# Attention and a gated layer on one core: weight conversion and gram matrices rearranged, order of work searched anew

## The chip, the cores and the metric

One core of a Trainium2 chip runs the whole program. The metric is device time in microseconds of one execution. Engines: PE (matrix multiplication, with its weight loads PEld), DVE (vector), ACT (scalar), POOL (GpSimd), SP (issues the DMAs).

## The reference

Causal attention for 4 batches of 12 heads, 448 positions and head width 64, then a gated two-layer network over the 1792 tokens:

```python
scores = scale * np.matmul(q, k.transpose(0, 1, 3, 2))      # scale = 1/sqrt(64)
scores = np.where(mask, -1000000000.0, scores)              # causal
attn = np.exp(scores - np.max(scores, axis=-1, keepdims=True))
attn = attn / (np.sum(attn, axis=-1, keepdims=True) + 1e-09)
attn_out = np.matmul(attn, v)
x = attn_out.transpose(0, 2, 1, 3).reshape(1792, 768)
h = x @ w_in                                                # w_in 768 x 2048
g = h * (1.0 / (1.0 + np.exp(-1.702 * h)))
return g @ w_out                                            # w_out 2048 x 768
```

w_in and w_out arrive as 64-bit floating-point words, q, k and v as 32-bit ones.

## The kernel before

**Tiling.** Each batch is cut into two blocks of rows (256 and 192 positions), eight blocks in all. Heads are worked in pairs ("units", six a block). For the first batch attention is computed in float32: k and q are turned on PE (`turn`, line 893), scores go to PSUM (line 412), the softmax runs strip by strip of 64 rows (`chunk`, lines 1112 and 1126), the probabilities are turned on PE (line 883) and multiplied with v (line 1268). Later batches use pairs of float16 values, high part and remainder, that DMA transposes turn. A block's result is `xT` (high part and remainder, line 477). The gated layer takes a block at a time: `h_slice` multiplies eight slices of w_in (256 columns each) with `xT`, three products each (line 412, tile `ps_h`), ACT takes the tanh (line 1362), DVE forms the gate (line 1367) and splits it into `gT`; `out_tile` multiplies `gT` with w_out (line 1405, tile `ps_o`).

**Weights.** Before a slice of w_in or a pair of row groups of w_out can be used, its 64-bit words are loaded and turned into float32 by four passes (`to_f32`): a scaling of the upper words (line 472 on ACT), the low 13 shifted bits (line 574 on DVE or 566 on ACT), the sign bit (line 588, DVE only), and their union with the shifted upper word (line 599, DVE). A gram matrix on PE gives squares whose largest value, found by `tensor_reduce` on DVE (line 628), yields a power of two as scale; the same instruction takes the maximum over all partitions once `all_max` has spread the column on PE. Then ACT or DVE writes the high part in float16 (lines 472 and 474) and DVE the remainder (line 477): eight pairs `wib`, sixteen pairs `wob`. Slices 0 to 2 of w_in are converted in two halves of 768 columns, slices 3 to 7 in one piece of 1536. Gram matrices of v of the first batch, of w_in and of w_out are built of blocks of 128 columns: two matmuls, each with 64 stationary and 128 moving columns.

**What sets the order.** The code records operations with costs by engine, buffers read and written (`Ops.add`). `Ops.order` plans a forward pass over the five engines with these costs, takes the finishing times, plans backward with noise added to them, and repeats this 600 times; `scored` rates a plan, and the best one becomes the order on every engine. Where an operation lists two engines the plan also chooses the engine. Tile's own scheduling is off (`manual_schedule`), so a changed cost or a changed search moves instructions on all engines.

Of the kernel before, what the change touches and what calls it, by code (L numbers as in the profile page):

```python
# [48 lines left out]
    va=2,  # L49
    ub=(0.0, 60.0, 122.92, 9.75),  # L50
    wi2=2.63,
    early=3,
)

SEED = 2
# [2 lines left out]
class Ops:  # L58
# [8 lines left out]
    ENGINES = ("SP", "PE", "ACT", "DVE", "POOL")  # L67
    HOP = 0.14
    SECOND = 1e5
    LOAD = 0.68  # L70
    DMA_START, DMA_END, DMA_DEPTH = 1.23, 1.6, 8
    ROWS = 0.195

# [24 lines left out]
        deps.discard(me)  # L98
        self.ops.append((costs, fn, sorted(deps), prio, dma))

    ROUNDS, STEPS, SPREAD = 600, 6, (0.0, 0.5, 1.0, 2.0)

    def order(self):
        rnd = Random(SEED)
        best = now = self.scored([o[3] for o in self.ops])
        bad = 0
        for _ in range(self.ROUNDS):
            spread = rnd.choice(self.SPREAD)
            now = self.scored(self.backward(now, spread, rnd))
            if now[0] < best[0]:  # L110
                best, bad = now, 0
            else:
                bad += 1
                if bad % self.STEPS == 0:
                    now = best
        Ops.last = best[0]
        return best[1]
# [24 lines left out]
            free[e] = end[i]  # L142
        return max(free.values())

    def backward(self, found, spread, rnd):
        _, result, fin = found
        n = len(self.ops)
        on = dict(result)
        key = [-fin[i] - (rnd.gauss(0.0, spread) if spread else 0.0) for i in range(n)]
        wait, left = [0] * n, [0.0] * n  # L150
        for o in self.ops:
            for d in o[2]:
                wait[d] += 1
        ready = {e: [] for e in self.ENGINES}
        free = dict.fromkeys(self.ENGINES, 0.0)
        coming = [(0.0, i) for i in range(n) if not wait[i]]
        heapify(coming)
        at, now, done = [0.0] * n, 0.0, 0
        while done < n:
            while coming and coming[0][0] <= now + 1e-9:  # L160
                _, i = heappop(coming)
                heappush(ready[on[i]], (key[i], i))
            moved = False
            for e in self.ENGINES:
                if free[e] > now + 1e-9 or not ready[e]:
# [20 lines left out]
        return [end - x for x in left]  # L186
# [110 lines left out]
def dve(n, ap=0, rate=1.042):  # L297
    return {"DVE": (rate * n + 68 + 61 * ap) / 1e3}
# [14 lines left out]
def kernel(  # L313
# [13 lines left out]
    P = 128  # L327
# [44 lines left out]
    cols = cp.tile([P, 176], F32, name="cols")  # L372
    waste = cp.tile([P, 512], BF16, name="waste")
    one16 = cp.tile([P, P], BF16, name="one16")
    ps_s, ps_s_r = bufs(2, [P, 512], F32, "ps_s", pp)
    ps_v = pp.tile([P, 2, 256], F32, name="ps_v")
    ps_h, ps_h_r = bufs(3, [P, 512], F32, "ps_h", pp)
# [12 lines left out]
    def col(tag, n=2, w=1):  # L390
        if tag not in col_at:
            col_at[tag] = (col_used[0], Ring(n))
            col_used[0] += n * w
            assert col_used[0] <= 175
        o, ring = col_at[tag]
        i = ring.next()
        return cols[:, o + i * w : o + (i + 1) * w], ("col", tag, i)
# [11 lines left out]
    def halves(out, lhsT, rhs, start, stop):  # L409

        for o in range(0, P, 64):
            nc.tensor.matmul(out[o : o + 64], lhsT[:, o : o + 64], rhs, start=start, stop=stop)  # L412

    def all_max(src, src_key, tag, turn, prio):

        if turn == "S":
            sb = ps_s_r.next()
            row, row_keys = ps_s[sb][:, :P], [("S", sb, x) for x in range(2)]  # L420
        else:
            row, row_keys = ps_o[1][:, :P], [("O", 1)]
        top = src.bitcast(BF16)[:, 1:2].to_broadcast([P, P])
        add(
            {"PE": 0.056},
            lambda e: halves(row, top, one16, True, True),
            [src_key, "one16"], row_keys, prio,
        )
        dst, key = col(tag + "_all", 2)
        gram_max(row, row_keys[0], dst, key, prio)  # L430
        return dst, key

    def norm_scale(tag, sq, sq_key, s, s_key, inv, inv_key, prio, near=False):
# [71 lines left out]


    def consts(e):
        nc.gpsimd.memset(one16, 1.0)
        nc.gpsimd.affine_select(
            out=one16, in_=one16, pattern=[[-1, P]], compare_op=ALU.is_equal, fill=0.0, base=0, channel_multiplier=1  # L510
# [40 lines left out]
    def to_f32(k, f, raw, raw_keys, dst, dst_keys, prio):  # L551
# [11 lines left out]
        def low(e):  # L563
# [9 lines left out]
            else:  # L573
# [12 lines left out]
        add(
            dve(n, rate=0.521),
            lambda e: nc.vector.tensor_scalar(
                out=words(dst, U16, 2)[..., 1],
                in0=words(raw, U16, 4)[..., 3],  # L590
                scalar1=0x8000,
                scalar2=None,
                op0=ALU.bitwise_and,
            ),
            raw_keys, dst_keys, prio,
        )
        add(
# [11 lines left out]
    def gram(x, keys, ps, ps_key, first, last, prio):  # L609


        t = x.bitcast(BF16).rearrange("p k (m n t) -> p k m n t", n=P, t=2)[..., 1]
        blocks = [(k, m) for k in range(t.shape[1]) for m in range(t.shape[2])]

        def mm(e):
            for k, m in blocks:
                halves(
                    ps[:, :P], t[:, k, m], t[:, k, m],
                    first and (k, m) == blocks[0],
                    last and (k, m) == blocks[-1],  # L620
                )

        add({"PE": len(blocks) * 0.0585}, mm, keys, [ps_key], prio)

    def gram_max(ps, ps_key, sq, sq_key, prio):
        add(
            dve(P),
            lambda e: nc.vector.tensor_reduce(out=sq, in_=ps[:, :P], axis=AX.X, op=ALU.max),
            [ps_key], [sq_key], prio,
        )  # L630

# [253 lines left out]
    def turn(src, r, keys, prio):  # L885
# [8 lines left out]
                        ps_t[64 * j : 64 * j + 64, o : o + r], src[:r, j, t], ident[:r, :r], start=True, stop=True  # L894
                    )

        add({"PE": 2 * (4 * r / 2.4 + 5) / 1e3}, mm, keys + ident_keys, [("T", h)], prio)
        return ps_t[:, 256 * h : 256 * h + 2 * r].rearrange("p (t x) -> p x t", t=2), ("T", h)

    def k_unit32(u, c0, c1, prio):  # L900
# [170 lines left out]
    def scores_of(n, u, run, qt, qt_key, prio):  # L1071
# [23 lines left out]
                        )  # L1095

        if f32(b, u):
            add({"PE": (4 * o / 2.4 + 6 * len(run)) / 1e3}, scores32, [qt_key] + kt_keys, bank(sb), prio)
        else:
            add(  # L1100
                {"PE": 2 * (o / 2.4 + 3 * len(run)) / 1e3}, scores, [qt_key] + kt_keys, bank(sb), prio
            )
# [52 lines left out]
    def p_turned(n, run, pi, pp_i, where, rs, r_key, prio):  # L1155
# [11 lines left out]
        for tiles in groups:  # L1167
# [6 lines left out]
            def mm(e, tiles=tiles, ps=ps, p0=p0):  # L1174
# [1 line left out]
                    flip_over(ps[:, (at - p0) * P : (at - p0 + 1) * P], z_of(i)[:, J])  # L1176

            add(
                {"PE": (nt * 60 + 2 * 93) / 1e3},
                mm,  # L1180
                ident_keys + [k for i in {t[3] for t in tiles} for k in z_keys(i)], [("H", hb)], prio,
            )
# [351 lines left out]
```

## Time and profile before

| | |
|---|---|
| runs shown | 603.24, 604.72, 606.03 us (median 604.72) |
| profiled execution | 605.29 us, span 603.5 us |
| PE, DVE, ACT, POOL busy | 575.1, 416.6, 351.6, 59.2 us |
| granted clock of TensorE, mean | 0.994 |

The span runs from the first to the last instruction of the profiled execution; its own time is 1.8 us longer. Matmuls are pipelined and their ends are modelled, so that PE's busy time counts overlapping matmuls once and says little about the rate; starts of consecutive groups do. DVE and ACT durations also overlap at their ends: the rows' durations add up to more than the busy time.

### The profile page before, as it was taken

Reading aid. Unit: us, or ns where it says so; the run is one execution under the profiler, and the core shown is the slowest. Engines: PE = TensorE matmul, PEld = TensorE weight load, DVE = VectorE, ACT = ScalarE, POOL = GpSimd, SP = SyncE. Lnnn points to the kernel's source line nnn. Section 1 sums busy time; section 2 is a strip of 40 time slices with the busy share of each in tenths; the row PEclk is TensorE's granted clock in tenths of the full one; section 3 lists DMA queues with packets and bytes.
Section 4 is the critical chain, followed back from the end, with each engine's and each line's share of the span. In section 5 each row is a group of like instructions: output and inputs, shape, how many; then the busy total and the mean of one; then the engine's idle time right before and its main releaser. Section 6 shows DMA issues by size and latency. Waiting matters only on the chain.

```text
span 603.5 us, 22259 instructions
## 1 busy us (share of the span) xinstructions
PE 575.1 (95%) x9526; PEld 501.7 (83%) x9526; DVE 416.6 (69%) x1164; ACT 351.6 (58%) x835; POOL 59.2 (10%) x162
## 2 busy tenths in 40 slices
PE   3876999999999999999999999999999999999997
PEld 2555867886699799977888899998999999889986
DVE  2999999999996889977489887978777122203100
ACT  4888899887866767754676465666355122203110
POOL 3000000012120121212111210211100000000000
PEclk9989899999999999999999999999999999999999
DMA  8998478554498987899997899575835400000000
GB/s 270 277 288 281 128 251 302 173 127 110 86 177 156 142 163 112 167 176 153 156 158 115 155 161 174 105 128 120 130 59 68 94 2 15 1 28 3 28 28 27
DMA packets 201604, 79.90 MB, mean 132 GB/s; under 512 B 182304, under 2 KB 191264, under 8 KB 201504
## 3 DMA queue, kind: packets, MB, share of 16 engines
q1 hardware_dynamic: 201504, 78.47, 61.5%
q8 instruction: 74, 1.21, 0.9%
q14 instruction: 26, 0.21, 0.1%
HBM read 41.68 MB, written 5.51 MB: 78 GB/s over the span
## 4 chain that ended last, share of the span: by engine, by line
PE 68%; DVE 4%; ACT 2%; DMA 1%; issue 1%; SPq 0%; DVEq 0%; ACTq 0%
PE ps_o L1405 33%; PE ps_h L412 26%; PE ps_s L1089 4%; PE ps_v L1268 4%; DVE z L1112 1%; DMA vraw<-in_v_dram 1%; ACT p L472 1%; PE ps_s L412 1%; DVE p L477 1%; PE ps_h L883 1%; DVE ps_h L1367 0%; ACT waste L462 0%; DMA kf<-in_k_dram 0%; DVE q L477 0%; DVE gT L477 0%
## 5 line engine op out<-in xcount | busy, mean ns | idle before, releaser
L412 PE MATMUL ps_h<-xT,wib 128*64 128x256 f16 (+1 forms) x4608 | 244.4, 260 | 0.1
L1405 PE MATMUL ps_o<-wob,gT 128*64 128x384 f16 x2688 | 239.8, 326 | 0.8 <-DVE wob L477 0.6
L412 PEld LDWEIGHTS <-wib 128*64 128x64 f16 x4608 | 226.3, 110 | 7.9 <-issue 2.1
L1405 PEld LDWEIGHTS <-gT 128*64 128x64 f16 x2688 | 171.8, 110 | 38.3 <-issue 3.2
L1126 ACT ACTIVATE z<-z,cols 128x320 f32<-128x320 f32 (+6 forms) x168 | 84.1, 501 | 51.6 <-DVE cols L1112 49.1
L1367 DVE SCALAR_TENSOR_TENSOR ps_h<-t,ps_h 128x512 f32<-128x512 f32 (+1 forms) x64 | 40.1, 626 | 82.4 <-ACT t L1362 82.0
L1362 ACT ACTIVATE t<-ps_h,cols 128x512 f32<-128x512 f32 (+1 forms) x64 | 40.3, 629 | 72.1 <-PE ps_h L412 68.0
L1112 DVE CUSTOM_DVE_ANT_0 z<-ps_s,mask,cols 128x128 f32<-128x128 f32 (+6 forms) x126 | 57.2, 479 | 18.0 <-PE ps_s L1089 17.4
L477 DVE SCALAR_TENSOR_TENSOR p<-z,cols,p 128x128 f16<-128x128 f32 (+3 forms) x126 | 63.2, 528 | 1.5 <-ACT p L472 0.8
L477 DVE SCALAR_TENSOR_TENSOR gT<-ps_h,gT 128x512 f16<-128x512 f32 (+1 forms) x64 | 39.7, 620 | 13.5 <-ACT gT L472 13.1
L1268 PE MATMUL ps_v<-PT,v 128*64 128x192 f16 (+7 forms) x792 | 44.7, 257 | 0.5 <-DVE cols L453 0.4
L1089 PE MATMUL ps_s<-kT,qT 128*64 128x64 f16 (+4 forms) x504 | 41.5, 273 | 1.2 <-DVE cols L1112 0.9
L472 ACT ACTIVATE p<-z,cols 128x384 f16<-128x384 f32 (+3 forms) x66 | 34.0, 533 | 13.3 <-DVE cols L1235 9.7
L472 ACT ACTIVATE gT<-ps_h 128x512 f16<-128x512 f32 (+1 forms) x53 | 28.9, 545 | 20.4 <-DVE ps_h L1367 20.3
L472 ACT ACTIVATE ob<-ps_o,cols 128x384 f32<-128x384 f32 x24 | 13.8, 577 | 45.0 <-PE ps_o L1405 44.6
L1126 ACT ACTIVATION_READ_ACCUMULATOR z<-z,cols 128x1 f32 x168 | 31.6, 188 | 0.0
L412 PE MATMUL ps_s<-kT,qT 128*64 128x320 f32 (+6 forms) x168 | 25.0, 409 | 5.6 <-DVE cols L1112 5.6
L1268 PEld LDWEIGHTS <-v 128*64 128x64 f16 x648 | 29.2, 110 | 1.0
L1089 PEld LDWEIGHTS <-qT 128*64 128x64 f16 x504 | 24.7, 110 | 4.3 <-issue 1.3
L1047 POOL TENSOR_SCALAR q<-q 128x512 f16<-128x512 f16 (+1 forms) x32 | 21.9, 686 | 50.8 <-ACT q L472 26.6
L474 DVE TENSOR_SCALAR p<-z,cols 128x256 f16<-128x256 f32 (+3 forms) x60 | 24.6, 422 | 1.3
L472 ACT ACTIVATE wob<-wob 128x768 f32<-128x768 f32 (+1 forms) x20 | 21.8, 1091 | 5.5 <-DMA wob<-in_moe_w_in_dram 5.0
(98 smaller groups left out, 564.9 us busy)
## 6 DMA issues: line engine op xcount, KB each, us to landing
wob<-in_moe_w_in_dram SPq DMA_DIRECT2D x16, 768.0 KB, 6.5
wob<-in_moe_w_out_dram SPq DMA_DIRECT2D x9, 768.0 KB, 6.2
vraw<-in_moe_w_out_dram SPq DMA_DIRECT2D x7, 768.0 KB, 6.7
out_dram<-ob SPq DMA_DIRECT2D x28, 192.0 KB, 2.2
kf<-in_k_dram SPq DMA_DIRECT2D x36, 112.0 KB, 3.3
vraw<-in_v_dram SPq DMA_DIRECT2D x9, 384.0 KB, 5.0
qf<-in_q_dram SPq DMA_DIRECT2D x48, 64.0 KB, 3.1
qf<-in_q_dram SPq DMA_DIRECT2D x48, 48.0 KB, 3.2
```

The costliest lines, as they stand in the source:

```text
L412: nc.tensor.matmul(out[o : o + 64], lhsT[:, o : o + 64], rhs, start=start, stop=stop)
L472: nc.scalar.activation(out=dst, in_=src, func=AF.Copy, scale=sc)
L474: nc.vector.tensor_scalar(out=dst, in0=src, scalar1=sc, scalar2=None, op0=ALU.mult)
L477: nc.vector.scalar_tensor_tensor(out=dst, in0=src, scalar=sc, in1=hi, op0=ALU.mult, op1=ALU.subtract)
L1047: nc.gpsimd.tensor_scalar(out=dst, in0=src, scalar1=1.0, scalar2=1.0, op0=ALU.mult, op1=ALU.mult)
L1089: nc.tensor.matmul(ps[64 * j : 64 * j + 64], qt[:, g, i - c0, 64 * j : 64 * j + 64], kt[:, : i + 1, 64 * j : 64 * j + 64], start=(g == 0), ...
L1112: lambda e: nc.vector.tensor_tensor_reduce(out=z[:, :w], in0=ps, in1=mask[:, S - w :], scale=c, scalar=3.0e38, op0=ALU.add, op1=ALU.min, a ...
L1126: lambda e: nc.scalar.activation(out=z[:, :w], in_=z[:, :w], func=AF.Exp, bias=m, scale=-1.0, accum_out=l),
L1268: nc.tensor.matmul(ps[64 * j : 64 * j + 64, 64 * (first - c0) : w], vt[:, J, j] if f32(b, u) else vt[:, gv, J, j, :], (p_f32(pi)[:, at] if ...
L1362: lambda e: nc.scalar.activation(out=th, in_=ph, func=AF.Tanh, scale=ts[:, sl : sl + 1]),
L1367: lambda e: nc.vector.scalar_tensor_tensor(out=ph, in0=th, scalar=1.0, in1=ph, op0=ALU.add, op1=ALU.mult),
L1405: nc.tensor.matmul(po[64 * j : 64 * j + 64, :OH], gT[:, f, gg, 64 * r : 64 * r + 64], wo_pair(f, gw, nh), start=(f == 0 and gg + gw == 0), ...
```

## The change

The sign pass of `to_f32` can be planned on ACT too (a copy of the scaled upper words to float16 in place of the masked bit). Gram matrices are built of blocks of 64 columns, and their maxima are taken over 64 columns. For k of the later batches and for w_out the maximum over partitions is replaced by a sum: PE multiplies a matrix of ones with the column, and the scale's first step reads the sum in PSUM. All slices of w_in are converted in two halves. The search has 800 rounds and puts noise on the finishing times of one stretch of the plan at a time; the costs of an issue on SP (0.68 to 0.5), of turns and of float32 scores on PE differ.

```diff
-    early=3,
+    early=8,
...
-    LOAD = 0.68
+    LOAD = 0.5
...
-    ROUNDS, STEPS, SPREAD = 600, 6, (0.0, 0.5, 1.0, 2.0)
+    ROUNDS, STEPS = 800, 3
+    WHOLE, STRETCH, SPREAD, EARLY = 30, (3.0, 6.0, 12.0, 25.0), (1.0, 2.0, 4.0, 8.0), 160.0
...
-        for _ in range(self.ROUNDS):
-            spread = rnd.choice(self.SPREAD)
-            now = self.scored(self.backward(now, spread, rnd))
+        for x in range(self.ROUNDS):
+            fin = now[2]
+            if x % 4 != 3:
+                if x < self.WHOLE:
+                    lo, hi, spread = 0.0, 1e9, rnd.choice((0.0, 0.5, 1.0, 2.0))
+                else:
+                    lo = rnd.uniform(-10.0, self.EARLY)
+                    hi, spread = lo + rnd.choice(self.STRETCH), rnd.choice(self.SPREAD)
+                fin = [f + rnd.gauss(0.0, spread) if lo < f < hi else f for f in fin]
+            now = self.scored(self.backward(now[1], fin))
...
+    def total(out, src):
+        for o in range(0, P, 64):
+            nc.tensor.matmul(out[o : o + 64], ones16, src, start=True, stop=True)
...
+        if tag in ("k", "wo"):
+            half = src.bitcast(BF16)[:, 1:2]
+            add(
+                {"PE": 0.03},
+                lambda e: total(row[:, :1], half),
+                [src_key, "one16"], row_keys, prio,
+            )
+            return row[:, :1], row_keys[0]
...
+        def sign(e):
+            if e == "ACT":
+
+                nc.scalar.activation(
+                    out=words(dst, F16, 2)[..., 1], in_=words(raw, F32, 2)[..., 1], func=AF.Copy
+                )
+            else:
...
         add(
-            dve(n, rate=0.521),
...
+            {**dve(n, rate=0.521), **act(n, rate=1.0)},
+            sign,
...
-                halves(
-                    ps[:, :P], t[:, k, m], t[:, k, m],
...
+                for o in range(0, P, 64):
+                    x = t[:, k, m, o : o + 64]
+                    nc.tensor.matmul(
+                        ps[o : o + 64, :64], x, x,
...
-    def gram_max(ps, ps_key, sq, sq_key, prio):
+    def gram_max(ps, ps_key, sq, sq_key, prio, n=64):
...
-        add({"PE": 2 * (4 * r / 2.4 + 5) / 1e3}, mm, keys + ident_keys, [("T", h)], prio)
+        add({"PE": (2 * (4 * r / 2.4 + 5) + 50) / 1e3}, mm, keys + ident_keys, [("T", h)], prio)
...
-                {"PE": (nt * 60 + 2 * 93) / 1e3},
+                {"PE": (nt * 109 + 150) / 1e3},
```

Line numbers of the changed kernel are higher: 412 became 420, the gram matmuls stand at 649, 472, 474 and 477 became 492, 494 and 497, 574 and 566 became 595 and 587, 588 became 614 (DVE) and 610 (ACT), 599 became 629, 628 became 659.

The first place is PE at the end of the first gram matrix of w_in. Before:

```order
L412 LDWEIGHTS wob
L412 MATMUL ps_o_98<-wob 64x128
L412 LDWEIGHTS cols
L412 MATMUL ps_o_98<-one_90,cols 64x128
L412 LDWEIGHTS cols
L412 MATMUL ps_o_98<-one_90,cols 64x128
L893 MATMUL ps_o_97<-ident,qf 64x128 x4
```

And now:

```order
L649 LDWEIGHTS wob
L649 MATMUL ps_o_98<-wob 64x64
L420 MATMUL ps_s_91<-kT_67,qT_77 64x64 x2
L420 MATMUL ps_s_91<-kT_67,qT_77 64x128 x2
L420 MATMUL ps_s_92<-kT_67,qT_77 64x192 x2
L420 MATMUL ps_s_92<-kT_67,qT_77 64x256 x2
```

The gram matmuls write 64 columns, and the first scores now stand between the gram matrix and the pair that spreads its maximum.

The second place is DVE around the third remainder of `xT` (block 0, the last that the first matmuls of h need). Before, from row 161 of DVE on:

```order
L439 TENSOR_SCALAR cols<-cols 128x1 x2
L477 SCALAR_TENSOR_TENSOR wib<-wob,cols,wib 128x6x256
L628 TENSOR_REDUCE cols<-ps_o_98 128x1
L446 TENSOR_SCALAR cols<-cols 128x1
L453 TENSOR_SCALAR cols<-cols 128x1 x2
L477 SCALAR_TENSOR_TENSOR xT_65<-ps_v,cols,xT_65 128x512
L628 TENSOR_REDUCE cols<-ps_o_98 128x1
```

Now, from row 149 on:

```order
L614 TENSOR_SCALAR wob<-wob 128x768
L659 TENSOR_REDUCE cols<-ps_o_98 128x1
L629 SCALAR_TENSOR_TENSOR wob<-wob 128x768 x2
L659 TENSOR_REDUCE cols<-ps_o_98 128x1
L473 TENSOR_SCALAR cols<-cols 128x1
L466 TENSOR_SCALAR cols<-cols 128x1
L459 TENSOR_SCALAR cols<-cols 128x1
L497 SCALAR_TENSOR_TENSOR xT_65<-ps_v,cols,xT_65 128x512
```

The remainder of `xT` moved from row 166 to row 156; the remainder of w_in's fourth slice (`wib`), which stood ahead of it, follows it now, and both conversions of a slice in halves lie before it.

The third place is ACT at the start of the program, where the first slices of w_in are converted. Before:

```order
L472 ACTIVATE wob<-wob 128x768
L566 ACTIVATE wob<-wob 128x768
L472 ACTIVATE qT_77<-ps_o_97 64x4x64
L472 ACTIVATE wob<-wob 128x768
L566 ACTIVATE wob<-wob 128x768
L472 ACTIVATE kT_67<-ps_o_97 128x256 x2
```

And now:

```order
L492 ACTIVATE wob<-wob 128x768
L587 ACTIVATE wob<-wob 128x768
L610 ACTIVATE wob<-wob 128x768
L492 ACTIVATE wob<-wob 128x768
L492 ACTIVATE qT_78<-ps_o_97 64x4x64 x2
L492 ACTIVATE wob<-wob 128x768
L587 ACTIVATE wob<-wob 128x768
L610 ACTIVATE wob<-wob 128x768
```

Seven of the 32 halves have their sign words on ACT (L610), six of them before the first tanh.

## Rows read from the trace of the kernel before

**Rows 1.** Stretch, length; busy us of PE, PEld, DVE, ACT, POOL; clock, DMA, GB/s.
```profile
0.00:20.00 20.00, 9.85 (x98) 7.49 (x98) 8.63 (x27) 10.99 (x23) 4.54 (x22) 1.00 0.92 279
20.00:70.00 50.00, 39.04 (x552) 28.51 (x552) 48.05 (x150) 41.76 (x99) 0.00 (x0) 0.93 0.90 264
70.00:130.00 60.00, 58.05 (x946) 48.63 (x942) 59.15 (x128) 56.89 (x102) 1.73 (x2) 1.00 0.61 200
130.00:157.10 27.10, 26.44 (x316) 18.03 (x314) 25.70 (x66) 22.23 (x50) 4.72 (x7) 1.00 0.54 105
157.10:300.00 142.90, 142.90 (x2550) 123.04 (x2548) 114.61 (x360) 94.15 (x258) 25.78 (x72) 1.00 0.89 154
300.00:400.00 100.00, 98.74 (x1736) 91.69 (x1733) 86.50 (x257) 64.18 (x171) 17.27 (x43) 1.00 0.87 147
400.00:603.50 203.50, 200.04 (x3354) 184.34 (x3349) 73.94 (x184) 61.40 (x136) 5.14 (x17) 1.00 0.24 47
```

**Rows 2.** Chain of waits: start, length in us, what, how many.
```profile
142.22 1.95 PE ps_o L1405 x24
...
516.81 22.43 PE ps_o L1405 x276
```

**Rows 3.** Waits of PE, 20 to 170 us, and of ACT, 105 to 160 us.
```profile
PE ps_s L412 <- DVE cols L1112: 5.6, 5, 1.6
PE ps_o L412 <- DVE cols L628: 3.3, 2, 1.9
...
ACT wob L472 <- DVE wob L477: 5.8, 6, 1.2
```

**Rows 4.** Timeline of DVE near 156 us: start, length, instruction.
```profile
156.13 1.01 DVE L477 SCALAR_TENSOR_TENSOR wob<-wob,cols 128x768 f16<-128x768 f32 x1
```

**Rows 5.** Timeline of PE at 112 and at 161 us.
```profile
112.18 0.51 PE L412 MATMUL ps_o<-wob 128*64 128x128 bf16 x12
112.53 0.71 PE L412 MATMUL ps_h<-xT,wib 128*64 128x256 f16 x10
...
160.73 0.34 PE L1089 MATMUL ps_s<-kT,qT 128*64 128x64 f16 x8
160.90 0.65 PE L1405 MATMUL ps_o<-wob,gT 128*64 128x384 f16 x6
```

**Rows 6.** DVE by shape: count | busy us, mean ns | idle before.
```profile
L588 DVE TENSOR_SCALAR wob<-wob 128x768 uint16<-128x768 uint16 x15 | 9.0, 607 | 0.3 <-ACT wob L472 0.3
...
L588 DVE TENSOR_SCALAR wob<-wob 128x1536 uint16<-128x1536 uint16 x5 | 5.2, 1045 | 0.0
...
L628 DVE TENSOR_REDUCE cols<-ps_o 128x1 f32<-128x128 f32 x22 | 6.2, 282 | 0.9 <-PE ps_o L412 0.6
...
L1112 DVE CUSTOM_DVE_ANT_0 z<-ps_s,mask,cols 128x128 f32<-128x128 f32 x18 | 6.2, 346 | 1.5 <-PE ps_s L1089 1.5
...
L1112 DVE CUSTOM_DVE_ANT_0 z<-ps_s,mask,cols 128x64 f32<-128x64 f32 x18 | 5.0, 278 | 2.7 <-PE ps_s L1089 2.7
...
L599 DVE SCALAR_TENSOR_TENSOR wob<-wob 128x768 int32<-128x768 int32 x15 | 14.1, 948 | 0.4 <-ACT wob L566 0.3
...
L599 DVE SCALAR_TENSOR_TENSOR wob<-wob 128x1536 int32<-128x1536 int32 x5 | 8.7, 1747 | 0.0
...
L474 DVE TENSOR_SCALAR PT<-ps_h 128x512 f32<-128x512 f32 x2 | 1.3, 672 | 0.0
...
L474 DVE TENSOR_SCALAR qT<-ps_o 64x192 f32<-64x192 f32 x3 | 1.1, 358 | 0.2
...
L1112 DVE CUSTOM_DVE_ANT_0 z<-ps_s,mask 128x448 f32<-128x448 f32 x6 | 3.7, 614 | 0.4 <-PE ps_h L883 0.4
```

**Rows 7.** Busy time from the start to the mark.
```profile
0.00:157.10 157.10, 133.37 (x1902) 102.65 (x1904) 141.53 (x367) 131.87 (x271) 10.99 (x31) 0.98 0.73 214
```

**Rows 8.** ACT by shape, the scaling of half a slice.
```profile
L472 ACT ACTIVATE wob<-wob 128x768 f32<-128x768 f32 x15 | 13.7, 914 | 5.5 <-DMA wob<-in_moe_w_in_dram 5.0 <-DMA wob<-in_moe_w_out_dram 0.5
```

**Rows 9.** Timeline of SP's queue, the first load of w_in.
```profile
1.72 0.43 SPq L648 DMA_DIRECT2D wob<-in_moe_w_in_dram  x1
```

More of the change, by code (lines that the diff above doesn't have):

```diff
@@ L143, in late, with backward @@
         return max(free.values())
-    def backward(self, found, spread, rnd):
-        _, result, fin = found
+    def backward(self, result, fin):
         n = len(self.ops)
         on = dict(result)
-        key = [-fin[i] - (rnd.gauss(0.0, spread) if spread else 0.0) for i in range(n)]
+        key = [-x for x in fin]
         wait, left = [0] * n, [0.0] * n
@@ L374 @@
     one16 = cp.tile([P, P], BF16, name="one16")
+    ones16 = cols[:, 174:175].bitcast(BF16)[:, 0:1].to_broadcast([P, 64])
     ps_s, ps_s_r = bufs(2, [P, 512], F32, "ps_s", pp)
@@ L393, in col @@
             col_used[0] += n * w
-            assert col_used[0] <= 175
+            assert col_used[0] <= 174
         o, ring = col_at[tag]
@@ L429, in all_max @@
         dst, key = col(tag + "_all", 2)
-        gram_max(row, row_keys[0], dst, key, prio)
+        gram_max(row, row_keys[0], dst, key, prio, P)
         return dst, key
@@ L507, in consts @@
     def consts(e):
+        nc.gpsimd.memset(cols[:, 174:175].bitcast(BF16), 1.0)
         nc.gpsimd.memset(one16, 1.0)
@@ L585, in to_f32 @@
         )
-        add(
-            dve(n, rate=0.521),
[L588 to L594, printed above, removed]
+        def sign(e):
[4 more added lines that the diff above has]
+            else:
+                nc.vector.tensor_scalar(
+                    out=words(dst, U16, 2)[..., 1],
+                    in0=words(raw, U16, 4)[..., 3],
+                    scalar1=0x8000,
+                    scalar2=None,
+                    op0=ALU.bitwise_and,
+                )
+        add(
+            {**dve(n, rate=0.521), **act(n, rate=1.0)},
+            sign,
             raw_keys, dst_keys, prio,
@@ L616, in mm @@
             for k, m in blocks:
-                halves(
-                    ps[:, :P], t[:, k, m], t[:, k, m],
-                    first and (k, m) == blocks[0],
-                    last and (k, m) == blocks[-1],
-                )
+                for o in range(0, P, 64):
+                    x = t[:, k, m, o : o + 64]
+                    nc.tensor.matmul(
+                        ps[o : o + 64, :64], x, x,
+                        start=first and (k, m) == blocks[0], stop=last and (k, m) == blocks[-1],
+                    )
         add({"PE": len(blocks) * 0.0585}, mm, keys, [ps_key], prio)
-    def gram_max(ps, ps_key, sq, sq_key, prio):
+    def gram_max(ps, ps_key, sq, sq_key, prio, n=64):
         add(
-            dve(P),
-            lambda e: nc.vector.tensor_reduce(out=sq, in_=ps[:, :P], axis=AX.X, op=ALU.max),
+            dve(n),
+            lambda e: nc.vector.tensor_reduce(out=sq, in_=ps[:, :n], axis=AX.X, op=ALU.max),
             [ps_key], [sq_key], prio,
@@ L1097, in scores_of @@
         if f32(b, u):
-            add({"PE": (4 * o / 2.4 + 6 * len(run)) / 1e3}, scores32, [qt_key] + kt_keys, bank(sb), prio)
+            add({"PE": (4 * o / 2.4 + 6 * len(run) + 30) / 1e3}, scores32, [qt_key] + kt_keys, bank(sb), prio)
         else:
```

## The prediction

> **What bounds the kernel now.** I read the busy table by stages first [rows 1]. It splits the run in two. Behind 157 us PE is busy 142.90 of 142.90 up to 300 and 98.74 of 100 up to 400; in the last row it is short by 3.46 us, in which the last output tile is scaled and stored. Before 157 us DVE is the full engine: 48.05 of 50, 59.15 of 60, 25.70 of 27.1, with ACT close behind from 70 us on (56.89 of 60). PE's busy time there (58.05 of 60) alone would not tell who leads, since ends of matmuls are modelled. So I asked for the rate of its matmuls: in the chain of waits 24 output matmuls take 1.95 us near 142 us, 81 ns each, and 276 of them take 22.43 us near 517 us, also 81 ns [rows 2]. Where PE has work it runs at its final rate; an earlier end comes only from less PE work or from less waiting. Who makes it wait stands in the list of waits of 20 to 170 us: DVE, by the score reduction (5.6 us) and the maxima of the gram matrices (3.3 us) [rows 3]. The mark at which this ends is DVE's sixteenth and last split of w_out, at 156.1 us [rows 4]; behind it the table shows PE without a gap. So the end moves with that mark, and with PE's work behind it.
>
> **The change part by part.** *Gram matrices.* 216 blocks (96 of w_in, 96 of w_out, 24 of v) are two matmuls each, now 64 moving columns wide instead of 128. Now: 12 of them, six blocks, start at 112.18 and the next group at 112.53, so 58 ns a block [rows 5]. A pair of 64 columns, each with its own weights: a group of two such pairs and two of 128 columns starts at 160.73 and the next at 160.90, so (170 - 2 x 58)/2 = 27 ns [rows 5], 22 to 32 with the rounding. Saved 30 ns a block, 6.5 us of PE in all; bounds 0 (the run of 12 or 24 blocks is longer than any 64-column run in the trace) and 7.8.
>
> The row speaks for half the time; one rule speaks against it. The Trainium skill ("TensorE: Matmul & The Clock Gate", section "LDWEIGHTS (loading the stationary operand)") prices a load by its columns over 1.2 GHz, 53 ns for 64. By it a block could not go under 53 ns and PE would be spared about 1 us. The 27 ns in the trace disagree for a run of two pairs; no row shows it for longer ones.
>
> *DVE before the mark.* I took the instructions that stand on DVE up to the sixteenth split, 366 before and 368 now, each at the duration of its own shape. Sign words: 22 x 0.607 + 5 x 1.045 = 18.6 us before, 25 x 0.607 = 15.2 now, -3.4; seven go to ACT [rows 6]. Maxima: 25 x 0.282 = 7.1 before; now 21, with 64 columns, which by the strips of 128 and 64 (346 against 278 ns) are worth 68 ns, so 21 x 0.214 = 4.5, -2.6 [rows 6]. Five slices in two parts: 10 x 0.948 - 5 x 1.747 for the last step and 10 x 0.607 - 5 x 1.045 for the low words (priced as sign words), +1.6 [rows 6]. The new order gives DVE two more halves of low words and three scalings of w_in at about 0.607, +3.0, and takes two PT copies (0.672) and three of qT (0.358) off it, -2.4; two late score strips fall behind the mark (0.614 and a little less), -1.2 [rows 6]. All others together +0.3. Sum -4.7. Durations overlap: the whole row list up to the mark sums to 170.0 us and DVE was busy 141.53 of them [rows 7], so one is worth 0.83: **-3.9 us**. Bounds: 0, if DVE only waits longer, and -5.6, the lead at the third xT remainder, which releases the first matmuls of h: 67.5 us of rows stand before it now, 60.8 after, 6.7 x 0.83.
>
> *PE beside it.* From 70 us on PE must give up 3.9 us as well. It has 1.95 + 0.66 us of idle there [rows 1], and the grams of one w_in slice and of w_out, 108 blocks, free 3.2: together 5.8, enough. PE's work left behind the mark is the same within 0.2 us. Before 70 us it waits 11 of 50 us, and its granted clock is 0.93 [rows 1]; should it be 0.86 with fewer columns to do, PE loses 3.5 us of full speed where it waits 11: I cost it at 0, at most 1.
>
> *ACT.* A sign half costs it 0.914, as the scaling of the same shape [rows 8], so 6.4 us. Six of the seven stand before the first tanh, and at that tanh ACT's rows sum to 1.3 us less than before, at the fifth to 2.8 less, because wib halves and scalings left it; 20 to 70 us have 8.2 us of idle ACT [rows 1]. At the eighth tanh (128 us) it is 6.6 more. There the cover is thinner: 3.1 us idle from 70 to 130 and 4.9 from 130 to 157, of which 5.8 are waits for DVE's own splits of w_out [rows 1, 3], and those shrink as DVE comes earlier. Cost 0; without the cover, the slower rival below.
>
> *Loads.* The half loads of w_in end seven rows earlier in SP's list; the second half of the first slice stands behind seven transfers in place of five, 2 x 0.43 = 0.9 us [rows 9]. DVE is idle 11.4 us of the first 20 [rows 1]: 0, else +0.9.
>
> *Scales from sums.* Nine k pairs and two w_out scales lose a maximum on DVE and a 128-column pair on PE. Behind the mark DVE has 28 us to spare up to 300, so the maxima are worth nothing; nine pairs on PE, 30 ns each, -0.3. The first shift now reads PSUM, which held its bank for the maximum before; nothing queues longer.
>
> Sum: -3.9 - 0.3 = -4.2 against the profiled execution, 605.29 us (span 603.5): 601.1. That execution lay 0.6 above the median of the runs shown, 604.72, so in those terms **600.5 us**. About 3 us, 0.5%, is what a measurement of this kernel can tell from no change.
>
> **The rivals.** *More is gained.* If the lead of 5.6 us at the third xT remainder is kept to the mark, PE can follow, since it has 5.8: -5.8 - 0.3, 598.6. For it: DVE leads the stage. Against: the row sums fall back to -2.4 at the eighth wib split and -4.7 at the mark. *The grams are paced by their weights.* If a block stays near its 58 ns because weights cannot come faster in a long run, PE follows only by its own 2.6 us of idle: -2.6, 602.1, no difference that can be told. For it the length of the runs, against it the 27 ns [rows 5]. The Trainium skill's price for a load, cited above, would lead here. *The new order trades one gap for another.* Its times come from a plan, and the profile shows what plans miss: PE idles 1.26 us between 300 and 400 us, where the next batch begins [rows 1]; there are three such places, and 0.8 us more at each undoes 2.4 of the 4.2: 602.9. *ACT takes the lead (slower).* Between the fifth and the eighth tanh ACT's rows grow from 2.8 less to 6.6 more. If its idle there cannot be filled because each gap is a wait with a fixed partner, the eighth tanh is late by 6.6 x 0.86 (ACT busy 131.87 [rows 7] of 153 us of rows) = 5.7 us, gT and the output matmuls with it, and DVE idles instead: 604.7 + 5.7 = 610.4. It decides as soon as ACT shows no idle time from 105 to 157 us and DVE over 4. Against it: six of seven sign halves lie before 70 us.
>
> **How the numbers follow.** Forecast (-3 to -5.5, 599 to 601.7) 0.42; more gained 0.15; grams paced 0.15; another gap 0.18; ACT leads 0.10. Faster by over 0.5%: 0.42 + 0.15 = 0.57. Within: 0.15 + 0.18 and 0.01 of the slow case, 0.34. Slower: 0.09. The range reaches from below the larger gain (596.5) to a little over no change (605.5): it leaves out nearly all of the ACT case and the outer end of the large gain.
>
> **What would show it.** In the profile after: groups of 12 gram matmuls with the next group 0.17 to 0.2 us behind their start (0.35 says paced by weights); the last split of w_out on DVE starting near 152 us, and DVE still over 95% busy from 20 us up to it; no idle PE from there to the end beyond 1 or 2 us. The forecast is wrong if the last split starts at 156 or later, if DVE shows idle time before it that it does not have now, or if PE idles over 3 us behind it.

## The result and the profile after

The changed kernel takes 597.06 us (median of 6 runs, 596.09 to 601.78), the kernel before 603.98 beside it: ratio 0.9892, 95% interval 0.9871 to 0.9913. It is faster, by 6.9 us where 4.2 were forecast. That is 1.1%, and the interval leaves out 1. The profiled execution took 596.57 us, span 594.8. The stages, with the columns of [rows 1]:

```profile
0.00:20.00 20.00, 9.52 (x122) 7.45 (x122) 9.20 (x29) 12.45 (x24) 4.47 (x23) 1.00 0.91 284
20.00:70.00 50.00, 40.56 (x616) 30.52 (x610) 48.44 (x161) 48.01 (x112) 0.00 (x0) 0.90 0.86 262
70.00:130.00 60.00, 56.18 (x934) 45.31 (x935) 59.14 (x130) 57.70 (x110) 2.21 (x4) 1.00 0.71 212
130.00:157.10 27.10, 26.94 (x310) 20.01 (x309) 24.79 (x73) 21.52 (x49) 5.60 (x11) 1.00 0.50 99
157.10:300.00 142.90, 142.90 (x2622) 124.89 (x2622) 114.80 (x353) 93.57 (x260) 23.78 (x68) 1.00 0.92 157
300.00:400.00 100.00, 100.00 (x1718) 85.67 (x1714) 84.78 (x252) 63.89 (x168) 18.28 (x48) 1.00 0.84 140
400.00:594.80 194.80, 191.34 (x3224) 159.43 (x3220) 66.66 (x166) 61.92 (x134) 2.90 (x9) 1.00 0.25 48
```

DVE is still the full engine from 20 to 130 us, ACT from 20 to 70 now fills with it (48.01, before 41.76), and PE has less to do from 70 to 130 (56.18, before 58.05). From 157 to 400 us PE shows no idle time; the 1.26 us of before are gone. The last split of w_out on DVE and the busy time up to its end, which answer [rows 4, 7]:

```profile
148.94 1.00 DVE L497 SCALAR_TENSOR_TENSOR wob<-wob,cols 128x768 f16<-128x768 f32 x1
```
```profile
0.00:149.94 149.94, 126.15 (x1898) 98.83 (x1900) 135.56 (x369) 133.22 (x276) 11.06 (x34) 0.97 0.77 224
```

The mark is 7.2 us earlier, against a span 8.7 us shorter (the profiled execution of before lay 1.3 us above its kernel's median, that of the changed kernel 0.5 below, so that the medians differ by 6.9). DVE's busy time up to it fell by 6.0 (141.53 to 135.56) and its idle time by 1.2 (15.6 to 14.4), while ACT is busier (133.22 against 131.87) in less time. The gram matrices on PE (start, length, answering [rows 5]):

```profile
113.90 0.36 PE L649 MATMUL ps_o<-wob 128*64 128x64 bf16 x12
114.09 1.15 PE L1436 MATMUL ps_o<-wob,gT 128*64 128x384 f16 x12
```

Six blocks in 0.19 us, 32 ns a block where it was 58. DVE and ACT by shape up to the mark (count | busy us, mean ns; answering [rows 6, 8]):

```profile
L629 DVE SCALAR_TENSOR_TENSOR wob<-wob 128x768 int32<-128x768 int32 x25 | 23.7, 960 | 0.6 <-ACT wob L610 0.5
...
L595 DVE TENSOR_SCALAR wob<-wob 128x768 uint16<-128x768 uint16 x22 | 13.3, 606 | 0.0
L614 DVE TENSOR_SCALAR wob<-wob 128x768 uint16<-128x768 uint16 x19 | 11.5, 611 | 0.0
L659 DVE TENSOR_REDUCE cols<-ps_o 128x1 f32<-128x128 f32 x9 | 2.5, 283 | 0.3 <-PE ps_o L420 0.3
L659 DVE TENSOR_REDUCE cols<-ps_o 128x1 f32<-128x64 f32 x11 | 2.4, 217 | 0.1
```
```profile
L492 ACT ACTIVATE wob<-wob 128x768 f32<-128x768 f32 x22 | 20.2, 919 | 6.2 <-DMA wob<-in_moe_w_in_dram 5.4 <-DMA wob<-in_moe_w_out_dram 0.7
...
L610 ACT ACTIVATE wob<-wob 128x768 f16<-128x768 f32 x6 | 6.4, 1065 | 0.0
```

A sign half takes ACT 1065 ns, not 914, and of the 21 maxima only eleven are 64 wide: ten that stand behind a product over partitions still read 128 columns (the nine of the row and one more in another bank). PE's waits of 20 to 170 us and ACT's of 105 to 160 (us, times, longest; answering [rows 3]):

```profile
PE ps_o L924 <- ACT qT L492: 3.5, 3, 2.0
PE ps_s L420 <- ACT kT L492: 2.4, 1, 2.4
PE ps_h L914 <- ACT z L492: 1.5, 3, 0.9
PE ps_s L420 <- DVE cols L1143: 1.3, 2, 0.8
```
```profile
ACT wob L492 <- DVE wob L497: 4.3, 4, 1.3
```

DVE's score reduction (L1143, before L1112) and the maxima held PE for 8.9 us; the reduction is left with 1.3, and ACT, with 7.4 in three rows, now stands ahead of it. ACT's own waits for the splits shrank from 5.8 to 4.3. Of the signs that the prediction named, the 0.19 us of the gram matrices, the busy DVE (97% from 20 us to the mark) and the PE without idle time from 157 to 400 us are there; the last split starts 3 us earlier than the 152 that it gave.

### The profile page after: what moved, and what is told of

Its sections match the earlier page's. It is cut to its first block, busy times and chain, and to the rows that moved or that the text cites. A ratio compares the mean times of both kernels' runs of the same rounds, so it can differ in the third digit from the quotient of the medians.

```text
span 594.8 us, 22263 instructions
## 1 busy us (share of the span) xinstructions
PE 567.4 (95%) x9526; PEld 473.3 (80%) x9526; DVE 407.8 (69%) x1157; ACT 359.1 (60%) x851; POOL 57.2 (10%) x163
## 4 chain that ended last, share of the span: by engine, by line
PE 76%; DVE 11%; ACT 7%; DMA 3%; issue 1%; SPq 1%; ACTq 0%
PE ps_o L1436 33%; PE ps_h L420 32%; PE ps_s L1120 5%; PE ps_v L1299 4%; DVE wob L497 2%; DVE wob L629 2%; DVE wib L497 1%; ACT z L1157 1%; ACT wob L492 1%; DMA wob<-in_moe_w_out_dram 1%; PE ps_o L924 1%; DVE z L1143 1%; ACT z L492 1%; DMA vraw<-in_moe_w_out_dram 1%; ACT PT L492 1%
## 5 line engine op out<-in xcount | busy, mean ns | idle before, releaser
L420 PE MATMUL ps_h<-xT,wib 128*64 128x256 f16 (+1 forms) x4608 | 241.3, 259 | 0.1
L1436 PE MATMUL ps_o<-wob,gT 128*64 128x384 f16 x2688 | 237.1, 326 | 0.6 <-DVE wob L497 0.6
L420 PEld LDWEIGHTS <-wib 128*64 128x64 f16 x4608 | 222.4, 110 | 10.1 <-issue 3.1
L1436 PEld LDWEIGHTS <-gT 128*64 128x64 f16 x2688 | 151.4, 110 | 57.6 <-issue 2.7
L1143 DVE CUSTOM_DVE_ANT_0 z<-ps_s,mask,cols 128x256 f32<-128x256 f32 (+6 forms) x126 | 57.1, 478 | 13.2 <-PE ps_s L1120 13.1
L497 DVE SCALAR_TENSOR_TENSOR gT<-ps_h,gT 128x512 f16<-128x512 f32 (+1 forms) x64 | 39.6, 619 | 12.7 <-ACT gT L492 12.4
L492 ACT ACTIVATE ob<-ps_o,cols 128x384 f32<-128x384 f32 x23 | 13.3, 579 | 53.8 <-PE ps_o L1436 53.4
L492 ACT ACTIVATE gT<-ps_h 128x512 f16<-128x512 f32 (+1 forms) x55 | 29.9, 543 | 22.7 <-DVE ps_h L1398 22.7
L1299 PE MATMUL ps_v<-PT,v 128*64 128x192 f16 (+7 forms) x792 | 42.3, 251 | 1.3 <-ACT PT L492 1.1
L492 ACT ACTIVATE p<-z,cols 128x256 f16<-128x256 f32 (+3 forms) x69 | 35.8, 539 | 11.8 <-DVE cols L1266 8.4
L494 DVE TENSOR_SCALAR p<-z,cols 128x128 f16<-128x128 f32 (+3 forms) x57 | 23.6, 427 | 1.3
L1078 POOL TENSOR_SCALAR q<-q 128x384 f16<-128x384 f16 (+1 forms) x29 | 20.1, 693 | 44.8 <-ACT q L492 30.1
L629 DVE SCALAR_TENSOR_TENSOR wob<-wob 128x768 int32<-128x768 int32 x25 | 23.7, 960 | 0.6 <-ACT wob L610 0.5
```

The costliest lines, as they stand in the source:

```text
L492: nc.scalar.activation(out=dst, in_=src, func=AF.Copy, scale=sc)
L494: nc.vector.tensor_scalar(out=dst, in0=src, scalar1=sc, scalar2=None, op0=ALU.mult)
L497: nc.vector.scalar_tensor_tensor(out=dst, in0=src, scalar=sc, in1=hi, op0=ALU.mult, op1=ALU.subtract)
L629: lambda e: nc.vector.scalar_tensor_tensor(out=words(dst, I32, 1)[..., 0], in0=words(raw, I32, 2)[..., 1], scalar=3, in1=words(dst, I32, 1 ...
L1143: lambda e: nc.vector.tensor_tensor_reduce(out=z[:, :w], in0=ps, in1=mask[:, S - w :], scale=c, scalar=3.0e38, op0=ALU.add, op1=ALU.min, a ...
L1299: nc.tensor.matmul(ps[64 * j : 64 * j + 64, 64 * (first - c0) : w], vt[:, J, j] if f32(b, u) else vt[:, gv, J, j, :], (p_f32(pi)[:, at] if ...
```

## The experiments

Two questions: which part makes the 7 us, and why it is more than forecast. The theory was the prediction's: DVE's row sets the mark, and each part is worth what it takes off that row. Its rivals: the shorter grams make the gain through PE; or the order alone makes it. Where an edit is made "in the fixed order", every engine's list is the changed kernel's except for the instructions named. All the rest is searched anew by the kernel's own planner. A ratio is to runs of the kernel before in the same round, whose median was 604.25 us for e1 to e4, 605.18 for e5 to e8 and 604.52 for e9 to e12, so ratios are to be compared and not medians. The changed kernel was timed once, beside 603.98; against it a difference of two ratios is good to 0.0025 or so, 1.5 us.

The table has, for the profiled execution of each, the start of the last w_out split on DVE (mark), DVE's busy and idle time up to that split's end, and the time that PE loses behind the mark: from start to start of its instructions, less what their columns take at the rate of the 81 ns matmuls [rows 2]. These columns are from one execution of each kernel; the last is an estimate whose differences, to about half a microsecond, say more than its level.

| kernel | median us | ratio to before (95%) | mark | DVE busy | DVE idle | PE lost behind |
|---|---|---|---|---|---|---|
| before | 603.98 | 1 | 156.1 | 141.6 | 15.6 | 2.7 |
| changed | 597.06 | 0.9892 (0.9871 to 0.9913) | 148.9 | 135.6 | 14.4 | 0.8 |
| e1 grams twice | 601.34 | 0.9949 (0.9936 to 0.9963) | 149.9 | 136.1 | 14.9 | 2.7 |
| e2 signs on DVE | 598.39 | 0.9899 (0.9886 to 0.9913) | 150.3 | 138.6 | 12.7 | 2.2 |
| e3 search of before | 601.67 | 0.9960 (0.9944 to 0.9977) | 156.7 | 137.6 | 20.1 | 1.0 |
| e4 new search alone | 605.13 | 1.0012 (1.0001 to 1.0023) | 154.1 | 139.7 | 15.4 | 3.3 |
| e5 grams of 128 | 598.38 | 0.9888 (0.9870 to 0.9905) | 149.5 | 136.8 | 13.7 | 0.8 |
| e6 maxima kept | 598.32 | 0.9887 (0.9868 to 0.9906) | 149.0 | 136.2 | 13.8 | 1.2 |
| e7 start number 3 | 601.19 | 0.9938 (0.9919 to 0.9958) | 146.4 | 133.1 | 14.4 | 5.1 |
| e8 start number 4 | 600.43 | 0.9932 (0.9913 to 0.9951) | 151.2 | 136.5 | 15.7 | 2.3 |
| e9 three undone | 602.07 | 0.9954 (0.9936 to 0.9972) | 154.4 | 141.1 | 14.2 | 1.3 |
| e10 slices whole | 602.49 | 0.9965 (0.9947 to 0.9983) | 155.2 | 136.0 | 20.2 | 0.9 |
| e11 start number 7 | 598.06 | 0.9908 (0.9882 to 0.9933) | 148.8 | 134.9 | 14.9 | 1.6 |
| e12 start number 17 | 600.34 | 0.9928 (0.9906 to 0.9950) | 151.0 | 137.0 | 15.0 | 2.8 |

### e1, each gram matmul twice (fixed order)

```
-                        start=first and (k, m) == blocks[0], stop=last and (k, m) == blocks[-1],
+                        start=first and (k, m) == blocks[0], stop=False,
+                    )
+                for o in range(0, P, 64):
+                    x = t[:, k, m, o : o + 64]
+                    nc.tensor.matmul(
+                        ps[o : o + 64, :64], x, x, start=False, stop=last and (k, m) == blocks[-1],
```

> The changed kernel with its order on every engine kept, but each 64-column gram matmul of w_in, w_out and v issued twice (the sums come out doubled, the scales follow): PE has 216 blocks x 32 ns = 6.9 us more before the mark, DVE and ACT the same work. If DVE leads the stage before the mark (the last split of w_out on DVE) and PE has room between its matmuls, the mark moves by 0 to 2 us and the time is 597 to 599. If PE leads there, all of it shows: 603 to 604, and most of the gain of the change is the shorter grams.

Measured: 0.9949, 3 to 4 us slower than the changed kernel, which lies between the two forecasts. The mark moved by 1.0 us only, while PE had about 6 us more work: that part was taken up by waiting. The rest shows behind the mark, where PE now waits for a remainder of gT on DVE, and DVE, just before that remainder, for a DMA that turns q (timelines of PE and of DVE, idle time in brackets):

```profile
173.89 0.85 PE L420 MATMUL ps_h<-xT,wib 128*64 128x192 f16 x16 [0.77 <-DVE gT L497]
```
```profile
172.88 0.49 DVE L494 TENSOR_SCALAR q<-qf,cols 128x512 f16<-128x512 f32 x1 [0.92 <-DMA qT<-q]
173.29 0.55 DVE L497 SCALAR_TENSOR_TENSOR gT<-ps_h,gT 128x384 f16<-128x384 f32 x1
```

In the changed kernel the same remainder starts at 171.13, behind no such wait. So what e1 loses behind the mark is a transfer that ends later, not columns of the gram matrices; why it ends later is open. e5 puts the same columns on PE in half the instructions and does not have it.

### e5, grams and maxima of 128 columns (fixed order)

```
-                for o in range(0, P, 64):
-                    x = t[:, k, m, o : o + 64]
-                    nc.tensor.matmul(
-                        ps[o : o + 64, :64], x, x,
...
+                halves(
+                    ps[:, :P], t[:, k, m], t[:, k, m],
+                    first and (k, m) == blocks[0], last and (k, m) == blocks[-1],
+                )
...
-            lambda e: nc.vector.tensor_reduce(out=sq, in_=ps[:, :n], axis=AX.X, op=ALU.max),
+            lambda e: nc.vector.tensor_reduce(out=sq, in_=ps[:, :P], axis=AX.X, op=ALU.max),
```

> The changed kernel with its order kept, gram blocks of 128 columns and maxima over 128 again: PE +5.6 us before the mark (216 x 26 ns), DVE 11 maxima 0.07 us longer each. From the doubled grams, where 6.9 us more PE work cost about 4, I expect 600 to 601.5: this part is the larger half of the gain. If the doubling hurt for another reason (a bank held longer, a chance of the late stage), 597 to 598.5.

Measured: 0.9888, no different from the changed kernel; the first forecast, that this part is the larger half of the gain, failed. Timeline of PE, and the busy time up to the mark:

```profile
113.73 0.52 PE L420 MATMUL ps_o<-wob 128*64 128x128 bf16 x12
114.08 1.14 PE L1434 MATMUL ps_o<-wob,gT 128*64 128x384 f16 x12
```
```profile
0.00:150.55 150.55, 130.12 (x1898) 104.10 (x1900) 136.82 (x369) 134.14 (x276) 11.06 (x34) 0.97 0.77 223
```

Six blocks take 0.35 us again, and PE is busy 4.0 us more up to a mark that is 0.6 later. So PE does not lead before the mark: with the other parts in place, what the shorter grams spare it, it waits.

### e2, the sign words back on DVE (fixed order)

```
-            if e == "ACT":
+            if e == "none":
```

> The changed kernel with its order kept, but the seven sign passes that stand on ACT issued on DVE at the same place of the order: DVE +7 x 0.61 = 4.3 us of rows, ACT -7 x 1.07 = 7.5 us. If DVE leads the stage before the mark, the mark comes 2 to 4 us later, 599 to 601. If PE leads or ACT does, the time is 595 to 597.5.

Measured: 0.9899, within the interval of the changed kernel and between the two forecasts. Busy time up to the mark:

```profile
0.00:151.32 151.32, 127.12 (x1898) 99.31 (x1900) 138.63 (x376) 127.34 (x269) 11.02 (x34) 0.97 0.75 222
```

Seven instructions of about 0.61 us added 3.1 us to DVE's busy time, 0.44 each, and moved the mark by 1.4: its idle time gave the other 1.7. A difference of 1.4 us between two executions is about what their times scatter by.

### e6, eleven maxima in place of the sums (fixed order)

```
-                lambda e: total(row[:, :1], half),
+                lambda e: halves(row, half.to_broadcast([P, P]), one16, True, True),
...
+            if tag in ("k", "wo"):
+                nc.vector.tensor_reduce(out=top1, in_=sq, axis=AX.X, op=ALU.max)
+                top = top1
```

> The changed kernel with its order kept, k and w_out scaled by the maximum over partitions again: 11 maxima of 0.28 us more on DVE, two of them before the mark, and a 128-column pair instead of a 1-column pair on PE. If DVE's work behind the mark is hidden, as my prediction had it, 597 to 597.8. If the idle PE at the batch borders went away because of the shorter k chain, 598.5 to 599.5 with PE idle again near 310 us.

Measured: 0.9887, mark within 0.1 us: the sums are worth nothing that can be told.

### e9, all three taken back at once (fixed order)

The edits of e2, e5 and e6 together.

> In the changed kernel's fixed order three edits are taken back at once: the seven sign words of ScalarE go to VectorE (no instruction left in their place on ScalarE), the gram matrices and their maxima are again 128 wide, and the eleven maxima of the queries', keys' and output weights' scales come back in place of the sums. What is left of the change is the order and the halves of the w_in slices. Theory A (VectorE's row sets the end of the early stage, so each edit is worth what it takes from that row, and the three add up): taken back one at a time they moved the last split by +1.4, +0.6 and +0.1 us; together 2 to 3 us, VectorE's busy time before the mark near 140 us, ratio 0.991 to 0.993. Theory B (each is hidden only while the others give slack; taken back together they meet): mark beyond 153 us, ratio 0.995 or more. Theory C (order alone makes the gain): ratio within 0.001 of the changed kernel's 0.989.

Measured: 0.9954, 3.7 us more than the changed kernel (0.0062 of 604.5), where the three differences one at a time sum to nothing (each of them good to about 1.5 us). Theory B of its expectation holds. Busy time up to the mark and in its part from 20 us on, and the mark:

```profile
0.00:155.35 155.35, 131.04 (x1898) 103.59 (x1900) 141.12 (x379) 128.14 (x269) 10.87 (x34) 0.97 0.74 216
20.00:155.35 135.35, 122.39 (x1802) 96.97 (x1802) 131.56 (x356) 118.04 (x250) 6.41 (x11) 0.96 0.72 208
```
```profile
154.35 1.00 DVE L503 SCALAR_TENSOR_TENSOR wob<-wob,cols 128x768 f16<-128x768 f32 x1
```

DVE's busy time rose by 5.6 and the mark by 5.4, while DVE's idle time stayed (14.2 against 14.4): here a microsecond of DVE is a microsecond of the mark. That fits DVE in the lead, as forecast: from 20 us to the mark DVE idles 3.8 us and PE 13.0. It does not settle it, since PE is busy 4.9 us more up to the mark as well, and no run takes back two of the parts. It also says that a test which undoes one part only cannot price it.

### e10, four slices converted whole again (fixed order)

```
+            def second(e):
+                seen[i] = not seen.get(i, False)
+                if not seen[i]:
+                    fn(e)
+
+            add(costs, second if whole else fn, reads, writes, prio)
...
+                    (NU, raw, wob[:, t * RG : (t + 2) * RG], seen) if s in (3, 4, 6, 7) else None,
```

> In the changed kernel's fixed order the w_in slices 3, 4, 6 and 7 are converted whole again: each of the four steps is one instruction of 1536 elements at the place of the later of its two halves, and the earlier place is empty (slice 5 keeps its halves). All else, the engine of the later half too, stays. Theory A (halves cost VectorE's row some 0.06 us for each extra instruction, forecast +1.6 us in all, and give nothing else): some twelve VectorE instructions fewer, last split 0.5 to 1 us earlier or unmoved, ratio 0.987 to 0.990. Theory B (halves let a step begin when the first transfer has landed, and that is worth more than their cost): VectorE idles 1 to 3 us more before the mark, last split 1 to 3 us later, ratio 0.991 to 0.995.

Measured: 0.9965, 4.4 us more than the changed kernel (0.0073 of 604.5), the largest of all in the fixed order. Theory B comes nearest, and its bounds are passed. Stages, one stretch of the second of them, and DVE's waits from 20 to 130 us:

```profile
20.00:70.00 50.00, 38.30 (x595) 29.54 (x593) 45.45 (x149) 45.20 (x107) 0.00 (x0) 0.90 0.88 265
70.00:130.00 60.00, 56.37 (x882) 44.95 (x880) 57.13 (x127) 56.27 (x102) 1.85 (x4) 0.94 0.62 193
```
```profile
76.50:83.30 6.80, 5.80 (x61) 4.29 (x63) 6.26 (x14) 5.29 (x12) 0.00 (x0) 0.50 0.73 199
```
```profile
DVE wib L497 <- ACT wib L492: 2.1, 3, 1.1
DVE wob L643 <- ACT wob L624: 1.4, 1, 1.4
DVE cols L673 <- PE ps_o L420: 1.3, 3, 0.5
```

DVE executes eleven instructions fewer and its durations sum to 163.3 us, 3.1 less than in the changed kernel; yet it is busy as long (136.0 against 135.6), and it idles 5.8 us more, 5.0 of them from 20 to 130 us, where the slices are converted. That a whole step makes the other engine wait for 1536 elements, and a half for 768, explains the wait for a sign word on ACT (L624, 1.4 us); the longest row, the remainders of `wib`, waits for high parts (L492) that are whole in both kernels, and it is not shown that the halves stand behind it.

Two things bound the 4.4 us. The order was searched with halves in it, so a plan made for whole slices would lose less; such a plan with all else changed was not run. And the granted clock is 0.50, the 1.2 GHz level, from 76.5 to 83.3 us, after two waits of PE of 1.3 us each, where the changed kernel has 1.00. By an estimate, 6.8 us at half clock cost PE up to 3.4. The times go with the mean clock: the five executions at 0.988 or more took 599.74 to 602.39 us, the six at 0.985 and 0.986 took 602.49 to 604.73. By the median of the five, 601.17, the loss is 3.2 us. Whether the clock fell because of the whole slices, or by itself, is not shown.

### e3 and e4, the two searches

e3 is the changed kernel with the search, the load price and the three PE prices of before:

```
-    ROUNDS, STEPS = 800, 3
+    ROUNDS, STEPS, SPREAD = 600, 6, (0.0, 0.5, 1.0, 2.0)
...
-    LOAD = 0.5
+    LOAD = 0.68
```

> All new instructions (sign on ACT allowed, grams of 64, sums, eight slices in halves), but the search and the planner's costs of the kernel before. By my row sums the instructions save DVE 1.4 and the re-assignment by the new order 3.3 of 4.7 us, and PE has 5.6 to 6.3 us less to do either way: if DVE leads, 601 to 603; if PE's work is what counts, 597 to 599.

e4 is the reverse: the kernel before with the new search and those four prices.

> The kernel before with the new search and the new costs and none of the new instructions. If the order is worth what is left after the instructions (DVE leads), 600 to 602; if PE's work is what counts, no gain: 603 to 605.

Measured: e3 0.9960, e4 1.0012. Neither half carries the gain, with one draw of its search for each. e3's 601.67 us lie in its forecast for a leading DVE. e4 gained nothing, as its forecast for PE's work had it, but its rows give another reason. Busy time up to the mark, of e3 and then of e4:

```profile
0.00:157.71 157.71, 130.89 (x1892) 100.59 (x1893) 137.56 (x368) 135.75 (x281) 10.43 (x34) 0.95 0.74 211
```
```profile
0.00:155.07 155.07, 133.65 (x1900) 105.55 (x1902) 139.68 (x362) 131.85 (x267) 11.61 (x33) 0.98 0.74 216
```

With the old search DVE is relieved of 4 us and idles 4.5 more (e3's profile is of its slowest execution, 604.96, at the lowest clock of the nine, so that its mark and its 4.5 may be too late and too large). With the new search alone DVE is relieved of 1.9 and the mark comes 2.0 earlier, but the time is no shorter: PE loses 3.3 us behind the mark, half of it in one place (PE's waits behind 157 us):

```profile
PE ps_s L419 <- ACT k L469: 1.6, 1, 1.6
```

### e7, e8, e11 and e12, the number that the search starts from

```
-SEED = 2
+SEED = 3
```

(4, 7 and 17 in the others.) Instructions, prices and rules stay; only the order found differs.

> The changed kernel with another seed of the search (3 for 2): same instructions, another order. If the order found is typical of the search, 596 to 598.5. If the order of the change is a lucky draw that explains why it gained more than its parts, 599 to 602.

> As the run before with seed 4: 596 to 598.5 if the order found is typical, 599 to 602 if it is a lucky draw. The spread of the three seeds also says how much of any re-planned comparison is the draw.

> The changed kernel with the search started from another number (7 in place of 2), instructions and costs unchanged: the order alone differs. Theory A (the surplus of the changed kernel over the forecast is the draw; other draws give about -4 us as 3 and 4 did): ratio 0.992 to 0.995, with 2 to 5 us of TensorE's time lost behind the mark or a later mark. Theory B (draws scatter evenly around the changed kernel's): ratio 0.986 to 0.991.

> As the run before it with 17: a fourth other draw. Theory A: ratio 0.992 to 0.995. Theory B: 0.986 to 0.991. If both of these runs lie below 0.990, the draw that the changed kernel has is an ordinary one, and the forecast's size was wrong for the instructions, not for the order.

Measured: 0.9938, 0.9932, 0.9908 and 0.9928. None beats the changed kernel; 7 cannot be told from it and lies in the range of an even scatter, while 3, 4 and 17 lie in the range of a lucky draw. The four average 0.9927, 4.4 us under before, and with the changed kernel's own number the five give 0.9920. The marks lie between 146.4 and 151.2, and PE's losses behind them between 0.8 and 5.1 us. e7 has the earliest mark of all and is the slowest of the five, for its gaps behind (PE's waits behind 157 us, e7, then e12):

```profile
PE ps_s L1120 <- DVE cols L1143: 2.0, 2, 1.7
PE ps_v L1299 <- DMA PT<-p: 0.9, 1, 0.9
```
```profile
PE ps_s L1120 <- DMA qT<-q: 1.0, 1, 1.0
PE ps_s L1120 <- DVE cols L659: 0.3, 1, 0.3
```

So the gain that the change has with an ordinary order is about 4.4 us, by four draws, and the changed kernel drew one that is 2 to 3 us better. Part of this spread goes with the granted clock, which differs between executions of one order: start number 7 took 597.5 to 598.1 us in the four executions with a mean clock of 0.993 or more, and 601.2 and 601.5 in the two at 0.987 and 0.989.

## Why the prediction was right, and where its sizes were off

The direction and the place were right: most of the gain lies before the mark. The size was not the one that it held likeliest: -6.9 us lies outside its -3 to -5.5 (chance 0.42), and what came about is its rival "more is gained" (0.15).

*DVE leads before the mark: right, as far as the runs tell the engines apart.* DVE's busy time and the mark move together when the whole of it changes: -6.0 and -7.2 from before to after, +5.6 and +5.4 in e9. The two tests that could have shown PE in the lead, e5 and the mark in e1, say no: 4.0 us more of busy PE in e5 moved the mark by 0.6, where 3.1 us more of busy DVE in e2 moved it by 1.4.

*DVE's row, -4.7 and -3.9 after overlap: the mis-sized term.* It measured -3.3 in durations (169.7 to 166.4), so less than counted, and -6.0 in busy time, so much more. Three parts. The maxima gave -1.9, not -2.6, since only eleven became narrow, where the prediction counted all 21. The halves were priced at +1.6 of durations times 0.83; by e10 they add 3.1 us of durations and no busy time. The factor itself is what changes: 0.834 before, 0.833 in e10, 0.815 in the changed kernel. And the forecast let idle time stand still; without the halves of four slices, in this order, DVE idled 5.8 us more, with the fall of the clock in it. I had priced the halves as a cost of about 1.3 us, and they are the part whose removal costs most, 3.2 to 4.4. In this order that step failed in sign, though not the sum; whether it fails in a plan made for whole slices is open.

*The lead would fall back from 5.6 to 3.9: wrong.* First h matmul 64.6 to 58.9, first output matmul 117.6 to 112.9, mark 156.1 to 148.9: a lead of 5.7, 4.7 and 7.2. Of the rivals it was "more is gained" that came nearest (598.6), and by its mechanism, the lead kept to the mark.

*PE can follow only because the grams shrink: half right.* The block came to 32 ns (forecast 27, with 22 to 32 as its bounds). The 53 ns by the price for a load of the Trainium skill's page cited in the prediction are not borne out by the run of twelve. But e5 follows without it, at no measurable cost. The rival of grams paced by their weights would therefore not have given 602.1 either: PE waits in more places before the mark than the 2.6 us of idle in the windows showed. Only with DVE's other relief gone too (e9) can the grams' parts show, and then as part of 3.7 us that these runs do not divide.

*ACT takes the signs at no cost: right, at another price.* 1065 ns, not 914, 7.5 us for seven. The cover held: ACT's idle time before the mark fell from 25.3 to 16.7 us, the waits for the splits from 5.8 to 4.3, and no row puts PE's or DVE's lost time on L610 beyond the 0.5 us shown above. Taken back alone, the relief of DVE is worth the 1.4 us of e2 at the mark, and nothing that can be told in the time.

*Behind the mark, -0.3: too small.* PE's losses there fell from 2.7 to 0.8 us, 1.9 of the 8.7 in the profiles; the sums, which the -0.3 stood for, are worth nothing (e6). The forecast had this place as a rival loss only. The other draws show it as both: 1.6 to 5.1 us. In the profiles the gain is then -7.2 at the mark, -1.9 behind it, and +0.4 of PE's work: behind the mark stand, above all, four float32 score matmuls and seven turns of z more, and sixteen output matmuls fewer. The prediction had this work equal within 0.2.

*The order.* The prediction took it as one order with given rows, and its 4.2 us is what four other orders of the same instructions average (4.4). That agreement is luck: the rows that it counted were those of this order. The 2.7 us by which the changed kernel beat the forecast is the size of that spread.

## What to carry to other kernels

Two engines that hand work back and forth are priced by what each waits for the other, not by the sum of their instructions: halving a step adds instructions and can still gain, and its price is read from a version without it, with the granted clock of both beside it. When the order comes from a search, run a few other draws before giving a difference of half a per cent to an edit, and undo edits together as well as singly, because slack hides any one of them.

## What the runs showed of the hardware that was not expected

- Pairs of 64-column bf16 matmuls with their own weights held 32 ns a block through runs of six blocks; the same blocks with 128 columns took 58.
- ACT takes 1065 ns for a half slice of f32 into every second 16-bit word, 919 ns for the same count of f32 into f32.
- On DVE seven more passes of 0.61 us cost 0.44 us of busy time each (e2), and the same slices in halves, 3.1 us more by their durations, cost 0.4 us less of it (the changed kernel against e10). It is no price of a pass: in e9, 5.0 us more of durations added 5.6 us of busy time.
- The granted clock from 20 to 70 us was 0.90 in the changed kernel and 0.97 with start number 7, with marks 0.1 us apart (e11):

```profile
20.00:70.00 50.00, 37.19 (x569) 26.64 (x567) 48.59 (x163) 48.34 (x113) 0.00 (x0) 0.97 0.92 265
```

These are two orders, and it does not follow that the clock is free. Within one order slower executions went with a lower mean clock where other orders were tried (e8: 599.1 to 600.1 us in the five at 0.991 and 0.994, 603.9 and 605.4 in the two at 0.985 and 0.983; e11 and e12 alike), while the kernel before took 604.0 to 605.8 us at 0.989 and 604.4 and 605.2 at 0.996 and 0.997 (the round of e1 to e4). What the clock costs in this stage is open.
